# Chunk 0's out-projection by 26 streamed products instead of Strassen's 28

## The chip, the core and the metric

The kernel runs on one core of a Trainium2 chip. Its engines are TensorE (PE, matmuls; PEld are its weight loads), VectorE (DVE), ScalarE (ACT), GpSimd (POOL) and SyncE (SP, which issues most DMAs). Each engine takes its instructions in order, and semaphores hold one engine for another. The metric is the device time of one execution in microseconds; lower is better.

## The reference

```python
scores = scale * np.matmul(q, k.transpose(0, 1, 3, 2))
scores = np.where(mask, scores, -1000000000.0)      # mask: q and k lie nearest the same of 16 centroids
attn = np.exp(scores - max) ; attn = attn / (sum + 1e-09)
x = np.matmul(attn, v)                              # 4 batches x 8 heads x 768 tokens x 64 -> 3072 x 512
h = x @ w_in                                        # 512 -> 2048
g = h * erf(softplus(h))
out = g @ w_out                                     # 2048 -> 512, float32
```

All inputs are float32; the two weights come to the core as 64-bit words (the kernel decodes them by itself, from pairs of 32-bit words).

## The kernel before, in words

**Attention.** Sixteen head pairs follow one another (`period(p, i)`, p = 0 to 15, six periods each). In each period PE does scores and the products with v, ACT the exponentials, DVE maxima and transposes, and POOL adds up the probabilities (`accumulate`). Beside that the weights are decoded, block by block ("steps" n of 32: 16 for `w_in`, 16 for `w_out`): a DMA fetches the raw words into a free tile, ACT takes size, rest and sign, DVE bounds and shifts, and POOL adds the two halves (`summed(n)`) and starts the fetch that reuses the place. Two steps go with a head pair; the last `N_LATE` steps come after the attention. In the last four pairs DVE and POOL also build linear combinations of `w_in` and of x (`forms`; `FORMS` gives DVE's, `POOL_FORMS` the pairs in which POOL takes some).

**MoE part.** The 3072 tokens are six chunks of 512. For each, the hidden layer is computed in two lots (`hidden(n, lot)`): four blocks of seven Strassen products each (`block`, order 1, 2, 6, 7, 5, 3, 4), two float32 matmuls of 128x128 by 128x256 to a product. `fresh` says how each product's bank is evicted into the tiles g: in a lot with the usual copy, ACT copies product 1 and DVE adds or subtracts all the others onto it, in order. PE writes to eight PSUM banks in turn (`bank()`), so it can be eight products ahead of the evictions. Chunks 2 to 5 use a form with 49 products for each pair of chunks (`hidden49`), whose right sides are stored in DRAM as `a_dram`: `begin49` stores parts of `w_in` there, `add49` adds other parts by accumulating DMAs that POOL issues, `copy49` copies one set.

**Out-projection.** Chunk 0 does it in two lots (`project(0, lot, pace)`), each of 2 x 7 Strassen products of four matmuls: 28 products. Chunk 1 and the later ones use `project26`: 26 products of four matmuls. Their right sides are blocks of `w_out` as they are, fixed sums kept in SBUF (`slot(i)`), and ten sums that are streamed from DRAM (`b_dram`, 512 KB each) through a ring of three tiles (`load_stream`), each load issued when the product three stream uses earlier has been given to PE. The left sides are sums of g tiles that DVE builds in place as the products go on (`LEFT_STEPS`), and `AFTER` says how each product is added into the output tiles. The sums of `w_out` blocks are made by POOL (`forms26`, in two pieces to a sum) and, where they are streamed, stored by a DMA.

**What sets the order.** Calls through `te`, `ve`, `ae`, `ge` and `sy` keep the program's order on PE, DVE, ACT, POOL and SP. DMAs issued through `nc.sync` may be placed elsewhere on SP's queue by the framework's planner. `aside_work` is a list of small jobs of which `block` takes `pace` after each product. Tiles from a pool with few buffers wait for the last reader of the buffer's former tile; `gp` has four g buffers, `actp` one buffer for the gate's curves, `gsp` four.

Chunk 0's sequence before: hidden lot 0, hidden lot 1, out-projection lot 0, chunk 1's hidden lot 0, out-projection lot 1, chunk 1's hidden lot 1 (`hidden26`), chunk 1's `project26`. POOL first makes Strassen's forms of `w_out` (`out_forms`) for chunk 0, and then, during chunk 1's hidden layer, twenty 26-product sums out of blocks and of those forms (`EARLY_FORMS`, `LATE_FORMS`).

Of the kernel before, what the change touches and what calls it, by code (L numbers as in the profile page):

```python
# [19 lines left out]
P = 128  # L20
# [5 lines left out]
HW = S // 2  # L26
# [17 lines left out]
POOL_FORMS = range(12, 16)  # L44
# [4 lines left out]
N_LATE = 10  # L49
# [5 lines left out]
EARLY_FORMS = [  # L55
# [3 lines left out]
]  # L59
LATE_FORMS = [  # L60
    (3, -6, 0, -1, None), (4, 0, 6, -1, None), (0, -7, 0, 1, 6), (7, -3, 0, -1, None),
    (10, -4, 2, -1, 0), (6, -6, 6, -1, None), (9, -2, 6, 1, 2), (8, -7, 1, -1, 5),
]
# [49 lines left out]
KEPT = {0: 10, 5: 11}  # L113
HELD = 11
N49 = 2
OUTER = (1, 2, 6, 5, 3, 7, 4)
OUT_ORDER = (1, 3, 2, 5, 4)
# [25 lines left out]
def kernel(  # L143
# [145 lines left out]
    for f in range(HF):  # L289
        for g in (f, HF + f):  # L290
            w_steps.append((w_out[:, g], moe_w_out[g * P : (g + 1) * P]))
# [5 lines left out]
    place_of = {n: places[n % PLACES] for n in range(N_EARLY)}  # L297
    after_of = {n: n + PLACES for n in range(N_EARLY - PLACES)}
    after_of.update({N_EARLY + n: N_EARLY + n + 4 for n in range(N_LATE - 4)})
# [8 lines left out]
    def late_places(first, places):  # L308
        for i, place in enumerate(places):
            place_of.update({N_EARLY + n: place for n in range(first + i, N_LATE, 4)})  # L310
            fetch(N_EARLY + first + i)
# [275 lines left out]
    def divide(u):  # L587
# [9 lines left out]
        if u + 1 < len(units):  # L597
            inv = routep.tile([P, QW], F32, name="inv")
            den = routep.tile([P, QW], F32, name="den")
        else:  # L600
            inv, den = part_of(0, 4 * HW, QW), part_of(1, 0, QW)
# [29 lines left out]
    def load_x(n):  # L631
        if n < NCHUNK:
            if n not in x_of:
                x_of[n] = xp.tile([P, DM // P, CT], F32, name="x_own")
            nc.sync.dma_start(
                out=x_of[n], in_=x_dram.rearrange("(k p) t -> p k t", p=P)[:, :, n * CT : (n + 1) * CT]
            )
# [25 lines left out]
    def coming(n):  # L663
        return range(n + 1, n + 3) if n < N49 else range(n + 2, min(n + 4, NCHUNK)) if n % 2 == 0 else ()
# [39 lines left out]
    def w_out_parts(f, n):  # L704
        f1, f2 = slice(f, f + n), slice(HF + f, HF + f + n)
        return (
            w_out[:, f1, 0:HM], w_out[:, f1, HM:], w_out[:, f2, 0:HM], w_out[:, f2, HM:],
            [more_out[:, i, f1] for i in range(3)],
        )

    g_of = {}
    sums_of = {}

    def g_parts(n, s, lot):
        g, new = g_of[n, s, lot], sums_of[n, s, lot]
        return (
            g[:, 0, :, 0:P], g[:, 1, :, 0:P], g[:, 0, :, P:], g[:, 1, :, P:],
            [new[:, i] for i in range(3)],
        )
# [50 lines left out]
    def further(c11, c12, c21, c22, u):  # L770
        return {
            1: [lambda m: ae.copy(out=u, in_=m), lambda m: onto(c11, m)],
            2: [lambda m: onto(c11, m)],
            6: [lambda m: onto(u, m), lambda m: onto(c12, u)],
            7: [lambda m: onto(u, m), lambda m: onto(c21, u)],
            5: [lambda m: onto(c12, m), lambda m: onto(u, m), lambda m: onto(c22, u)],
            3: [lambda m: onto(c12, m)],
            4: [lambda m: minus_of(c21, c21, m)],
        }

# [34 lines left out]
    def gate(n, lot, s):  # L815

        g = g_of[n, s, lot].rearrange("p h j t -> p (h j t)")
        box = []

        def curves():  # L820
            t = actp.tile([P, 2 * FG * HT], F32, name="a_s")
            box.append(t)
            ae.activation(out=t, in_=g, func=ACT.Softplus)
            ae.activation(out=t, in_=t, func=ACT.Erf)

        def product(i):
            c = slice(i * 512, (i + 1) * 512)
            ve.tensor_tensor(out=g[:, c], in0=box[0][:, c], in1=g[:, c], op=ALU.mult)

        return curves, [functools.partial(product, i) for i in range(2 * FG * HT // 512)]  # L830

    def add_hidden(n, lot, s):
        sums_of[n, s, lot] = gsp.tile([P, 3, FG, P], F32, name="g_more")
        return left_forms(ve, *g_parts(n, s, lot))

    def idle(n):
        return [lambda: None] * n

    def gates(n, lot, which=(0, 1), between=()):
        work = list(between)  # L840
        for s in which:
            curves, products_of = gate(n, lot, s)
            if s == which[0]:
                work = [curves] + work + idle(7 - len(work)) + products_of
            else:
                work += [curves, *sums, *idle(3)] + products_of
            sums = add_hidden(n, lot, s)
        return work + sums
# [4 lines left out]
    def project(n, lot, pace):  # L853

        w = rights(*w_out_parts(lot * FG, FG))
        for s in range(2):
            if lot == 0:
                osb_of[n, s] = outp.tile([P, 2, DM], F32, name="osb")
            osb = osb_of[n, s]
            g = lefts(*g_parts(n, s, lot))  # L860
            c = osb[:, 0, 0:HM], osb[:, 0, HM:], osb[:, 1, 0:HM], osb[:, 1, HM:]

            def done(i):
                if not lot:
                    return
                if (n, s) == (NCHUNK - 1, 1):
                    t, cols = {3: (0, slice(0, DM)), 5: (1, slice(HM, DM)), 4: (1, slice(0, HM))}.get(i, (None, None))
                else:
                    t, cols = {3: (0, slice(0, DM)), 4: (1, slice(0, DM))}.get(i, (None, None))
                if t is not None:  # L870
                    nc.sync.dma_start(out=out_v[2 * n + s, :, t, cols], in_=osb[:, t, cols])

            after = further(*c, up.tile([P, HM], F32, name="u")) if lot else fresh(*c)
            block(lambda i: [(g[i][:, f], w[i][:, f]) for f in range(FG)], after, done, pace)
            del g_of[n, s, lot], sums_of[n, s, lot]


    ring, extra, more_room = [], [], []
    a_dram = dram.tile([len(OUTER), 7, P, LC], F32, name="a_dram")
    b_dram = dram.tile([N_STREAM + len(KEPT), P, FG * HM], F32, name="b_dram")  # L880
# [25 lines left out]
    def place26(x, f):  # L906
        if x == HELD:
            return extra[f // 2].rearrange("p j t -> p (j t)").rearrange("p (f m) -> p f m", f=2)
        return (slot(x) if x >= 0 else w_block(-1 - x))[:, f : f + 2]

    def forms26(steps):
        work = []
        for o, a, b, sign, k in steps:
            form = plus_of if sign > 0 else minus_of

            def piece(f, o=o, a=a, b=b, form=form, k=k):
                form(place26(o, f), place26(a, f), place26(b, f), ge)
                if k is not None:
                    stored = b_dram[k].rearrange("p (f m) -> p f m", f=FG)
                    if o == HELD:  # L920
                        nc.sync.dma_start(out=stored[:, f : f + 2], in_=place26(o, f))
                    elif f:
                        nc.sync.dma_start(out=stored, in_=slot(o))

            work += [functools.partial(piece, f) for f in (0, 2)]
        return work

    def load_kept(i):
        nc.sync.dma_start(out=slot(i), in_=b_dram[KEPT[i]].rearrange("p (f m) -> p f m", f=FG))
# [43 lines left out]
    def hidden26(n, lot, generation=()):  # L973
        generation = list(generation)
        first_steps = [functools.partial(left_step, n, x) for x, step in enumerate(LEFT_STEPS) if step[0] < 0]

        def paired(work):
            if not generation:
                return work
            both = []  # L980
            for w in work + idle(14 - len(work)):
                g = generation[:1]
                del generation[:1]
                both.append(lambda w=w, g=g: [f() for f in (w, *g)])
            return both

        def middle():
            finish_aside()
            aside_work.extend(paired(gate_work(n, lot, 0, first_steps if lot else ())))

        if lot and n > 1:
            aside_work.extend(paired(gate_work(n, 0, 1)))
        else:
            aside_work.extend(paired([]))
        hidden(n, lot, {1: middle})
        finish_aside()
        for work in generation:
            work()
# [18 lines left out]
    def begin49(o):  # L1017
        for a, part in w49_parts(*{1: (0, 0), 2: (0, 1), 4: (1, 1)}.get(o, (1, 0))):
            nc.sync.dma_start(out=form49(o)[:, a], in_=part)

    def copy49(o, source):
        nc.sync.dma_start(out=a_dram[OUTER.index(o)], in_=a_dram[OUTER.index(source)])
# [697 lines left out]
```

## Time and profile before

| | |
|---|---|
| median of the runs | 950.82 us |
| the profiled execution | 950.97 us |
| its span, from first to last instruction | 949.2 us |
| PE, DVE, POOL, ACT busy | 941.6, 752.9, 557.5, 554.8 us |
| granted clock of TensorE, mean | 1.000 |

Among the runs behind the median is one of 1956.87 us; the other two are 950.82 and 950.69. A profile page gives, for each engine, its busy time; then the chain of work that ended last; then groups of instructions as "line engine operation out<-in, shapes, count | busy us, mean ns | idle time before them and what ended it". Nearly all instructions have line L134, since one helper records them, so they are told apart by their tiles: `bank` and `turned` are PSUM banks, `g` the hidden layer, `a_s` the gate's curves, `g_more` and `more_out` places of `w_out` sums, `x_own` a chunk of x, `a_dram` and `b_dram` the two stores in DRAM. A view by stretches gives each engine's busy time between two times in us from the span's start, the clock, the DMA engines' share and GB/s. A view of the DMAs gives, for each queue, packets, MB and share; q1 carries what SP issues, q0 what POOL issues.

### The profile page before, as it was taken

What the parts mean: (1) busy time and instruction counts of PE and PEld (TensorE: products, weight loads), DVE (VectorE), ACT (ScalarE), POOL (GpSimd) and SP (SyncE); (2) the same over time, 40 slices, a digit from 0 to 9 for tenths busy, and PEclk for the clock granted to TensorE, in tenths of its full rate; (3) what the DMA queues carried; (4) which work ended last, traced back from release to release, by engine and by line L of the source; (5) the groups of instructions that cost most, each with busy time, mean ns of one, the idle gap of its engine ahead of it and who ended that gap; (6) DMA issues with size and microseconds to landing.
All of it is one profiled execution on the core that took longest, in us unless ns stands there. A gap on an engine that the chain in (4) does not pass through costs nothing.

```text
span 949.2 us, 20906 instructions
## 1 busy us (share of the span) xinstructions
PE 941.6 (99%) x8167; PEld 695.6 (73%) x8167; DVE 752.9 (79%) x1310; ACT 554.8 (58%) x852; POOL 557.5 (59%) x381
## 2 busy tenths in 40 slices
PE   8999999999999999999999999999999999999998
PEld 3555555555555555588888888888888888888887
DVE  8888888888888887788879878456786974768977
ACT  3788888888887665557523542357825225675341
POOL 1688888888888888845779930576600028770000
PEclk9999999999999999999999999999999999999999
DMA  9444544647454314292895486556645435533443
GB/s 208 93 114 107 116 108 109 156 113 200 91 113 107 71 34 146 81 326 67 164 192 212 155 238 216 156 155 175 191 141 182 156 112 154 171 97 114 153 133 111
DMA packets 181730, 136.15 MB, mean 143 GB/s; under 512 B 131808, under 2 KB 141536, under 8 KB 181600
## 3 DMA queue, kind: packets, MB, share of 16 engines
q1 hardware_dynamic: 174416, 125.21, 45.9%
q0 software_dynamic: 4720, 9.18, 5.5%
q8 instruction: 65, 1.06, 0.5%
q10 hardware_dynamic: 2496, 0.43, 0.2%
q14 instruction: 33, 0.27, 0.1%
HBM read 95.72 MB, written 40.89 MB: 144 GB/s over the span
## 4 chain that ended last, share of the span: by engine, by line
PE 97%; DVE 1%; DMA 0%; ACT 0%; issue 0%; DVEq 0%
PE bank L134 45%; PE turned L134 30%; PE sc L134 17%; PE wide L134 6%; DVE nmx L134 1%; DMA pr<-in_centroids_dram 0%; DMA in_q<-in_q_dram 0%; DVE pr L134 0%; ACT pr L134 0%; DVE sims L134 0%; DVE qT L134 0%; ACT qm L134 0%; DVE turned L134 0%; DVE wide L134 0%; ACT km L134 0%
## 5 line engine op out<-in xcount | busy, mean ns | idle before, releaser
L134 POOL TENSOR_TENSOR more_out<-more_out,pr 128x768 f32<-128x768 f32 x128 | 222.4, 1738 | 17.5 <-ACT pr L134 9.7
L134 DVE TENSOR_REDUCE nmx<-wide 128x2 f32<-128x512 f32 (+2 forms) x189 | 180.7, 956 | 57.8 <-PE wide L134 56.8
L134 ACT ACTIVATE pr<-sc 128x768 f32<-128x768 f32 x192 | 148.6, 810 | 71.5 <-PE wide L134 63.9
L134 PE MATMUL turned<-pr,in_v 128*32 128x193 f32 x3072 | 144.9, 330 | 0.0
L134 PEld LDWEIGHTS turned<-pr,in_v 128*32 128x32 f32 x3072 | 91.5, 109 | 51.5 <-issue 25.5
L134 PE MATMUL sc<-qT,kT 64*128 64x384 f32 x528 | 98.7, 487 | 0.0
L134 POOL TENSOR_TENSOR more_out<-pr,pr 128x768 f32<-128x768 f32 x32 | 58.7, 1834 | 46.6 <-ACT pr L134 46.6
L134 POOL TENSOR_TENSOR u<-w_in 128x1 f32<-128x1 f32 x2 | 0.4, 189 | 138.6 <-DVE w_in L134 138.6
L134 PE MATMUL bank<-x_own,more_in 128*128 128x256 f32 x280 | 69.1, 379 | 0.0
L134 PE MATMUL bank<-g_more,more_in 128*128 128x256 f32 x288 | 66.5, 380 | 0.0
L134 PE MATMUL wide<-kv,qv 64*128 64x256 bf16 (+2 forms) x378 | 64.2, 328 | 1.3 <-DVE nmx L134 0.7
L134 DVE TENSOR_TENSOR g<-g 128x512 f32<-128x512 f32 x70 | 48.6, 695 | 19.3 <-PE bank L134 12.3
L134 PE MATMUL wide<-km,qm 64*128 64x256 bf16 (+3 forms) x378 | 62.6, 327 | 0.0
L134 PEld LDWEIGHTS sc<-qT,kT 64*128 64x128 f32 x528 | 48.0, 187 | 19.5 <-ACT inv L134 3.2
L134 PEld LDWEIGHTS bank<-g_more,more_in 128*128 128x128 f32 x288 | 54.6, 190 | 8.2 <-DVE g L134 0.8
L134 PEld LDWEIGHTS bank<-x_own,more_in 128*128 128x128 f32 x280 | 53.2, 190 | 7.2
L134 DVE TENSOR_TENSOR g<-g,bank 128x256 f32<-128x256 f32 (+1 forms) x85 | 41.9, 511 | 20.4 <-PE bank L134 12.7
L134 ACT ACT_TABLE_LOAD x36 | 46.2, 1283 | 18.4 <-DVE g L134 17.8
L134 PE MATMUL bank<-w_out,g 128*128 128x256 f32 x240 | 55.2, 379 | 0.0
L134 DVE TENSOR_TENSOR g<-a_s,g 128x512 f32<-128x512 f32 x56 | 51.8, 941 | 2.7 <-ACT a_s L134 2.7
L134 PEld LDWEIGHTS <-qv 64*128 64x128 bf16 x384 | 22.8, 93 | 41.4 <-issue 25.3
L134 ACT ACTIVATE x_own<-x_own 128x512 int32<-128x512 uint32 (+2 forms) x52 | 52.7, 1028 | 0.0
(253 smaller groups left out, 2148.3 us busy)
## 6 DMA issues: line engine op xcount, KB each, us to landing
more_in<-a_dram SPq DMA_DIRECT2D x98, 256.0 KB, 2.7
g_more<-b_dram SPq DMA_DIRECT2D x48, 512.0 KB, 3.6
x_own<-in_moe_w_in_dram SPq DMA_DIRECT2D x13, 512.0 KB, 3.6
in_v<-in_v_dram SPq DMA_DIRECT2D x32, 192.0 KB, 3.1
x_dram<-more_out SPq DMA_DIRECT2D x128, 48.0 KB, 2.5
a_dram<-w_in SPq DMA_DIRECT2D x12, 512.0 KB, 5.0
x_own<-x_dram SPq DMA_DIRECT2D x6, 1024.0 KB, 5.9
in_k<-in_k_dram SPq DMA_DIRECT2D x59, 96.0 KB, 2.7
```

The costliest lines, as they stand in the source:

```text
L134: ins = getattr(self.engine, name)(*args, **kw)
```

## The change

Chunk 0 takes the same way as chunk 1: `hidden26(0)`, `hidden26_second(0)`, `project26(0)`, and then `hidden26(1)`, `hidden26_second(1)`, `project26(1)`.

- The sums of `w_out` are now 18, all out of raw blocks and of one another: eleven in `FIRST_FORMS` beside chunk 0's hidden layer (22 pieces on POOL, all first pieces before all second ones) and seven in `LAST_FORMS` during `project26(0)`, at its products -1, 3, 5, 6 and 8. `out_forms`, `EARLY_FORMS` and `LATE_FORMS` go, and the kept copies with them. Two sums that are only streamed are made in the tile that chunk 1's x will take (`BESIDE`).
- `N_LATE` is 6 instead of 10: four more decodings lie in head pairs 12 and 13. POOL's eight forms of pairs 12 to 15 lie in 14 and 15. Four of the late steps' raw words go into two g tiles (`two_g`).
- x of chunk 1 is loaded after product 14 of `project26(0)`, together with x of chunk 2; before, it was loaded during the attention.
- The stores of `a_dram` are issued through `sy`, so in written order: sets 6, 5, 7 in `hidden26_second(0)` behind the stores of the first sums, 1, 2, 4 in `hidden26(1)`. The accumulating DMAs stand behind `project26(0)` in the program and behind POOL's last piece on POOL.
- `project26` has one way for all chunks: the first three evictions wait until product 3, and the gate's curves and products follow `plan26` in halves of the token columns, with x_own of the chunk as a second curve buffer.

```diff
-POOL_FORMS = range(12, 16)
+POOL_FORMS = range(14, 16)
-N_LATE = 10
+N_LATE = 6
-OUT_ORDER = (1, 3, 2, 5, 4)
+BESIDE = (11, 12)
+OUT_ORDER = (0, 1, 3, 2, 5, 4)
...
-            if i % HJ == 1 and p in POOL_FORMS and forms:
+            if i % HJ and p in POOL_FORMS and forms:
                 forms.pop(0)[1]()
...
-            nc.sync.dma_start(out=form49(o)[:, a], in_=part)
+            sy.dma_start(out=form49(o)[:, a], in_=part)
...
+    def hidden26(n, between={}, beside=(), **kw):
+
+        def middle():
+            aside_work.extend(abreast((gate_work(n, 0, 0), 1), (beside, 2)))
+
+        hidden(n, 0, {1: middle, **between}, **kw)
+
+    def hidden26_second(n, between={}):
 
         def middle():
             finish_aside()
+            aside_work.extend(first_steps26(n))
+
+        aside_work.extend(gate_work(n, 0, 1))
+        hidden(n, 1, {1: middle, **between})
         finish_aside()
...
+        last_forms = {p: sum((forms26([step]) for step in LAST_FORMS[p]), []) if not n else [] for p in LAST_FORMS}
+        run(f() for f in curves.get(-1, []) + last_forms[-1])
...
-            if p == 5 and n < N49:
-                load_x(n + 2)
+            if p == 14 and n < N49:
+                if n == 0:
+                    load_x(1, sy)
+                load_x(n + 2, sy)
...
-    late_places(2, [outp.tile([P, 2, DM], F32, name="osb").rearrange("p h m -> p (h m)") for _ in range(2)])
+    take_places(4)
+    two_g = [gp.tile([P, 2, FG, HT], F32, name="g").rearrange("p h j t -> p (h j t)") for _ in range(2)]
+    late_places(2, [t[:, i : i + 2 * LC] for t in two_g for i in (0, 2 * LC)])
...
-    hidden(0, 0, {0: finish_attention, 3: store(1)})
-    hidden(0, 1, {0: store(2), 1: store(4), 2: begin}, pace=2, first=ve.tensor_copy)
-    project(0, 0, 3)
-    hidden(1, 0, first=ve.tensor_copy)
-    project(0, 1, 3)
-    hidden26(1, 1, making)
-    project26(1)
+    making = forms26(FIRST_FORMS)
+    half = len(making) // 2
+    aside_work += idle(3) + abreast((sum((weights(n) for n in range(N_LATE)), []), 2), (idle(4) + making[:half], 1))
+    hidden26(0, {0: finish_attention}, making[half:], first=ve.tensor_copy)
+    hidden26_second(0, {0: store(6), 2: store(5), 3: store(7)})
+    project26(0, gates26(0))
     run(f() for f in add49(6, 1, 1) + add49(5, 1, 1) + add49(7, 0, 0) + add49(6, 0, 0))
+    hidden26(1, {0: store(1), 2: store(2), 3: store(4)}, first=ve.tensor_copy)
     copy49(3, 6)
+    hidden26_second(1)
+    project26(1, gates26(1))
```

More of the change, by code (lines that the diff above doesn't have):

```diff
@@ L309, in late_places @@
         for i, place in enumerate(places):
-            place_of.update({N_EARLY + n: place for n in range(first + i, N_LATE, 4)})
+            place_of[N_EARLY + first + i] = place
             fetch(N_EARLY + first + i)
@@ L813, in hidden @@
             between.get(j, lambda: None)()
[L815 to L830, printed above, removed]
@@ L850 @@
     out_v = out.rearrange("(n t p) m -> n p t m", p=P, t=2)
     osb_of = {}
[L853 to L875, printed above, removed]
@@ L912, in forms26, with piece @@
         work = []
[L913 to L925, printed above, removed]
-        return work
-    def load_kept(i):
-        nc.sync.dma_start(out=slot(i), in_=b_dram[KEPT[i]].rearrange("p (f m) -> p f m", f=FG))
+        for f in (0, 2):
+            for o, a, b, sign, k in steps:
+                def piece(f=f, o=o, a=a, b=b, form=plus_of if sign > 0 else minus_of, k=k):
+                    form(place26(o, f), place26(a, f), place26(b, f), ge)
+                    if k is not None:
+                        stored = b_dram[k].rearrange("p (f m) -> p f m", f=FG)
+                        sy.dma_start(out=stored[:, f : f + 2], in_=place26(o, f))
+                work.append(piece)
+        return work
     def load_stream(k, queue=nc.sync):
@@ L1283, in hidden49 @@
             load_stream(next_out + i)
[L1284 to L1295 removed]
+        first, second = (plan26({t: gates_of[tb, 1, t] for t in range(2)}) for tb in (1, 0))
         first[0][-1] = products_at(1, 0, 1, (1, 1), (0, 0), (1, 0), (0, 1)) + first[0][-1]
@@ L1634, in weights @@
         ]
-    def all_weights(lo, hi):
-        return sum((weights(n) for n in range(lo, hi)), [])
-    out_forms = [right_forms(ge, *w_out_parts(f, 2)) for f in range(0, HF, 2)]
-    def together(a, b):
-        work = []
-        while a or b:
-            work += a[:1] + b[:1]
-            del a[:1], b[:1]
-        return work
-    def begin():
-        for o in (6, 5, 7):
-            begin49(o)
-    def store(o):
-        return functools.partial(begin49, o)
-    aside_work += idle(3) + all_weights(0, 4) + out_forms[0] + out_forms[1]
```

193 lines of the change are left out of this document (61 added, 132 removed), and 3 rows, old and new, of the table EARLY_FORMS.

## The prediction

> **What bounds the kernel now.** I read the page first, for the busy shares and the chain that ended last.
>
> ```profile
> PE 941.6 (99%) x8167; PEld 695.6 (73%) x8167; DVE 752.9 (79%) x1310; ACT 554.8 (58%) x852; POOL 557.5 (59%) x381
> PE 97%; DVE 1%; DMA 0%; ACT 0%; issue 0%; DVEq 0%
> ```
>
> TensorE (PE) is busy for 99% of the span, and the chain runs over it for 97%. Next I cut the span at the first matmul of each head pair and of each block of the MoE part, and asked for busy time by stretch.
>
> ```profile
> core 0: us, PE busy (x) PEld busy (x) DVE busy (x) ACT busy (x) POOL busy (x), PEclk, DMA share, GB/s
> 285.70:310.00 24.30, 24.30 (x358) 13.63 (x355) 20.82 (x34) 19.28 (x33) 20.16 (x13) 1.00 0.47 110
> 310.00:334.20 24.20, 24.20 (x358) 13.57 (x356) 19.82 (x31) 15.40 (x28) 19.65 (x13) 1.00 0.34 67
> 381.90:404.80 22.90, 22.90 (x342) 12.98 (x338) 18.80 (x22) 13.66 (x23) 20.55 (x13) 1.00 0.29 96
> 404.80:429.80 25.00, 25.00 (x125) 21.49 (x122) 20.52 (x45) 11.96 (x15) 11.39 (x9) 1.00 0.86 308
> 429.80:454.00 24.20, 24.20 (x113) 21.06 (x111) 21.91 (x43) 18.28 (x19) 12.59 (x10) 1.00 0.14 45
> 454.00:478.30 24.30, 24.30 (x113) 21.38 (x113) 19.84 (x41) 15.84 (x12) 17.70 (x14) 1.00 0.98 190
> 575.20:620.10 44.90, 44.90 (x210) 39.52 (x209) 29.70 (x59) 13.08 (x27) 16.85 (x12) 1.00 0.51 164
> ```
>
> The rows are head pairs 11, 12 and 15, then chunk 0's two hidden halves (from 404.8), its first half out-projection (454.0) and chunk 1's 26-product out-projection (575.2 is its start). PE fills every stretch at a clock of 1.00. So the kernel gains only by fewer matmuls, and each new PE wait is added in full. The question is what the changed order makes PE wait for.
>
> **The change, part by part. 1: fewer products.**
>
> ```profile
> 457.61 1.89 PE L134 MATMUL bank<-more_out,g_more 128*128 128x256 f32 x8
> 459.34 1.89 PE L134 MATMUL bank<-w_out,g 128*128 128x256 f32 x8
> ```
>
> A product of the out-projection is eight matmul rows, and starts follow each other by 459.34 - 457.61 = 1.73 us. Chunk 0 goes from 28 to 26 products: 2 x 1.73 = **-3.45 us**. The built order has 16 matmul rows less, so this term is sure.
>
> **2: decoding and block sums in the last head pairs.** Four decodings move into pairs 12 and 13. Those become like pair 11, which holds two and takes 24.3 us beside 24.2 for pair 12: +0.1 each. The eight POOL forms that pairs 12 to 15 share now all lie in 14 and 15.
>
> ```profile
> L134 POOL TENSOR_TENSOR w_out<-w_out 128x512 f32<-128x512 f32 x10 | 14.6, 1470 | 0.0
> L134 POOL TENSOR_TENSOR more_out<-w_out,more_out 128x512 f32<-128x512 f32 x10 | 14.4, 1455 | 0.3
> L134 POOL TENSOR_TENSOR w_out<-w_out,more_out 128x512 int32<-128x512 int32 x6 | 7.8, 1297 | 12.2 <-ACT w_out L134 4.8 <-DMA x_dram<-more_out 3.6 <-DVE w_out L134 2.7
> 406.31 2.01 POOL L134 TENSOR_TENSOR more_out<-more_out,pr 128x768 f32<-128x768 f32 x1
> 413.11 1.31 POOL L134 TENSOR_TENSOR w_out<-w_out,more_out 128x512 int32<-128x512 int32 x1 [4.78 <-ACT w_out L134]
> 418.01 1.30 POOL L134 TENSOR_TENSOR w_out<-w_out,more_out 128x512 int32<-128x512 int32 x1 [3.59 <-DMA x_dram<-more_out]
> ```
>
> Two more forms of some 1.3 us in pair 15 make POOL 20.55 + 2.6 = 23.2 us of 22.9. PE's sums over the softmax wait for POOL's accumulates, so some of it shows: I take **+1.5 us** for the four pairs (bounds 0, if the probability buffers cover it, and 3, if half of the four moved forms' 5.2 us and a DVE delay show).
>
> **3: POOL is late, and holds chunk 0's hidden half.** POOL used to have ten late weight sums and eight forms in the first 48 us of the MoE part. Now it has six sums and 22 pieces of block sums there, and 14 more pieces behind them. In the built order the last weight sum stands behind five sums and ten pieces. From 415 us (the first sum's 413.11, later by the two extra forms of pair 15 less some slack), with the 3.6 us wait that the rows show before the second sum, it ends at 415 + 3.6 + 6 x 1.30 + 10 x 1.46 = 441. The raw words of the last four weight blocks lie in the two g buffers that the second half of the hidden layer writes first. That half begins at 404.8 + 1.5 + 24.2 + 1.3 (a hiccup at the start, of which 25.0 beside 24.2 us shows 0.8 today) = 432. VectorE (DVE), which works in order, is held at its first eviction into such a buffer, till 441. PE has eight banks, and a hidden product is half an out-projection product, 0.86 us: cover 6.9 us. Behind DVE's held instruction stand the gate products that free the curve buffer, and behind those ACT's next curves:
>
> ```profile
> 540.00 0.37 ACT L134 COPY g<-turned 128x256 f32<-128x256 f32 x1 [5.85 <-PE turned L134]
> 540.39 1.28 ACT L134 ACT_TABLE_LOAD   x1
> 541.69 2.01 ACT L134 ACTIVATE a_s<-g 128x1024 f32<-128x1024 f32 x2
> 543.71 1.28 ACT L134 ACT_TABLE_LOAD   x1
> 545.01 2.01 ACT L134 ACTIVATE a_s<-a_s 128x1024 f32<-128x1024 f32 x2
> 546.92 0.35 ACT L134 COPY g<-turned 128x256 f32<-128x256 f32 x1
> ```
>
> That is the group as it runs today in chunk 1: 546.92 - 540.39 = 6.5 us between two copies, covered by the banks alone. In chunk 0 it starts late: 441 + two or three gate products (2.5) + 6.5 = 450, and only then comes ACT's copy of the next block's first product, on which all that block's evictions hang. That product ends at 432 + 7 x 0.86 + 0.9 = 439; eight banks carry PE to about 445.5. Stall: some 4.5 us. Then DVE has to catch up beside a POOL that never rests, and this costs:
>
> ```profile
> L134 DVE TENSOR_TENSOR g<-a_s,g 128x512 f32<-128x512 f32 x11 | 16.1, 1483 | 1.2 <-ACT a_s L134 1.2
> L134 DVE TENSOR_TENSOR g<-g 128x512 f32<-128x512 f32 x11 | 7.6, 687 | 1.1 <-PE bank L134 1.0
> ```
>
> The first row is of 500 to 551 us, where POOL is busy throughout, the second of 575 to 620: 1.48 against 0.69 us for an SBUF-to-SBUF operation of one size. About 17 such stand between the hold and POOL's end: +13.5 us of DVE work, of which DVE's idle quarter hides most. I take 2.5 us. With the hiccup of 1.3 us (the x forms on DVE meet POOL's late accumulates, which now end later) this step is **+8.5 us**; bounds 1 (POOL some 5 us earlier, all covered) and 12. The Trainium skill, "SBUF — State Buffer", section "SBUF: two separate sides", says that the pair of ports which these two engines share is an exclusive lock for a whole instruction. If each of the 17 waited for a whole piece, DVE would take 0.69 + 1.46 = 2.15 us for each and the work would grow by 25 us, which would put the time near 978; the mean of 1.48 says that about half of it is waited for.
>
> **4: accumulating DMAs meet the loads.** Chunk 0's out-projection now streams ten 512 KB right sides and, after its product 14, loads x of chunks 1 and 2, 1 MB each. Both x loads used to come elsewhere (chunk 1's during the attention). And POOL issues the twelve accumulating DMAs as soon as its pieces are done.
>
> ```profile
> x_own<-x_dram SPq DMA_DIRECT2D x6, 1024.0 KB, 5.9
> 453.27 0.38 SPq L635 DMA_DIRECT2D x_own<-x_dram  x1
> 499.33 0.59 SPq L1022 DMA_DIRECT2D a_dram<-a_dram  x1
> q0 software_dynamic: 3776, 7.34, 98.5%
> q0 software_dynamic: 285, 0.56, 60.3%
> q1 hardware_dynamic: 300, 0.87, 47.7%
> g_more<-b_dram SPq DMA_DIRECT2D x48, 512.0 KB, 3.6
> g_more<-b_dram SPq DMA_DIRECT2D x3, 512.0 KB, 6.6
> q1 hardware_dynamic: 883, 2.37, 95.1%
> ```
>
> Today SP issues nothing between 453.27 and 499.33 us, and in 458 to 500 the accumulates (q0) have the engines to themselves: 7.34 MB in about 39 us. The next two rows are 567 to 572 us, where three accumulates meet loads: 285 packets against 300, so packets alternate. The load's median goes from 3.6 us to 6.6 (560 to 574). Alone, q1 moved 2.37 MB between 551 and 558. Now the new place. The out-projection starts at 432 + 24.2 + 7 = 463. POOL's first 22 pieces and six sums end at 415 + 3.6 + 7.8 + 22 x 1.46 = 458.5, its last 14 at 479, with a wait for a slot 480.5: there the accumulates begin, to last beyond 519. Product 14 ends at 463 + 15 x 1.73 = 489, so the x loads are issued into the middle of them. At alternating packets of 2 KB the loads get 300 packets x 2 KB in 5 us = 0.12 MB/us: 2.1 MB take 17 us, and stream block 8, queued behind, some 3 more, after a start of 2: landed at 511. PE needs it at product 22, 463 + 22 x 1.73 = 501. Stall 10 us. Block 4, whose sum POOL makes only after the out-projection has begun, is stored and reloaded just about when product 13 wants it: 2 to 4. I take **+14 us**; bounds 2 (loads at the rate of the last row, 7 us for all) and 25 (they get nothing until the accumulates end). The stores that SP now issues in written order, behind the last of the first block sums, only move this by some us.
>
> **The sum** is made against the profiled execution, 950.97 us (span 949.2 and 1.8 around it), 0.15 above the median of 950.82: -3.45 + 1.5 + 8.5 + 14 = +20.5, so **971.5 us**.
>
> **Rivals.** *Everything is covered, and only the matmuls count:* POOL reaches its last weight sum before 438, so that DVE's hold ends inside the 6.9 us of banks, and the x loads pass the accumulates. Then 951.0 - 3.45 = 947.5, faster. For it speaks that PE lost nothing in 500 to 551 with POOL always busy; against it, that nothing there waited for a late POOL result. *POOL's chain alone:* steps 2 and 3 as forecast, but the loads run as fast as between 551 and 558 and land before product 22: 951.0 - 3.45 + 1.5 + 8.5 = 957.5, up to 960 with block 4. *Starved loads:* the x loads wait until the accumulates end at 520 or later; the stall is 25 us or more, the time 983 to 995. *The change doesn't take effect:* 951; the built order speaks against it.
>
> **How the numbers follow.** Forecast 0.70, with 958 to 986 as its own range; all covered 0.12; POOL's chain alone 0.12; starved 0.05; no effect 0.01. Leaving out the first rival, no effect and most of the starved case, the range is 953 to 986. A measurement of this kernel tells about 2%, 19 us, from no change; that bound lies at 970, just under the forecast. Slower: six tenths of the forecast's 0.70 and the starved case, 0.48. Within 2%: all others, 0.51. Faster by 2% can't come from 3.45 us: 0.01.
>
> **What would show it.** Step 1: the out-projection's PE row count is 208 in chunk 0. Step 2: the last four pairs take 24.3, 24.3, 24 and 23.5 us. Step 3: PE idles near 445 us with ACT or DVE as releaser, and DVE has a gap that POOL's int32 sum ends. Step 4: PE idles 10 us or more about product 22, released by a DMA of g_more or by x_own, and the 1 MB loads land after 15 us and not 5.9. I am wrong if chunk 0's out-projection takes 45 us as chunk 1's does, or if POOL's last piece lies before 470.

## The result, and the profile after

The changed kernel takes 980.3 us, the kernel before 951.0 in the same comparison: a ratio of 1.0304, 95% interval 1.028 to 1.0327. Each of the two medians counts one far slower run (1617.2 and 1956.87 us); without it the changed kernel has a median of 979.35 (978.7 to 981.2) and the kernel before 950.82, and the ratio is taken without it. That is **slower by 3%**, on the side that the forecast of 971.5 pointed to, 8 to 9 us beyond it and inside the range.

The page's rows for PE and for the chain that ended last, to be laid beside 941.6 us (99%) and 97% of before:

```profile
PE 946.5 (97%) x8151; PEld 694.1 (71%) x8151; DVE 753.6 (77%) x1320; ACT 557.4 (57%) x880; POOL 531.8 (54%) x360
PE 45%; DVE 5%; ACT 3%; DMA 2%; POOL 2%; issue 1%; DVEq 0%; ACTq 0%; POOLq 0%
```

PE has 16 matmul rows less and is busy 5 us longer, in a span that is 28.4 us longer (977.6 beside 949.2). The chain now leaves PE: DVE, ACT, a DMA and POOL hold it for some time each.

Next, busy time by stretch, cut at the first matmul of head pairs 14 and 15, lots 0 and 1 of chunk 0's hidden layer (its two halves; columns as in the prediction), chunk 0's out-projection and chunk 1's:

```profile
358.40:382.10 23.70, 23.70 (x349) 13.17 (x346) 16.71 (x25) 13.91 (x26) 21.30 (x15) 1.00 0.19 43
382.10:406.50 24.40, 23.22 (x343) 12.88 (x339) 18.17 (x23) 13.65 (x24) 21.37 (x14) 1.00 0.16 54
406.50:434.80 28.30, 26.27 (x125) 21.07 (x122) 22.94 (x44) 20.82 (x24) 21.82 (x16) 1.00 0.32 117
434.80:468.90 34.10, 27.46 (x114) 21.82 (x113) 25.63 (x41) 7.85 (x10) 33.71 (x24) 0.95 0.44 168
468.90:529.40 60.50, 47.97 (x209) 40.76 (x208) 40.74 (x77) 20.11 (x35) 25.59 (x20) 0.92 1.04 274
577.80:624.20 46.40, 45.37 (x210) 39.41 (x209) 37.76 (x74) 18.65 (x34) 4.43 (x4) 1.00 0.64 187
```

Before, PE filled every such stretch at a clock of 1.00. Now it is short of work in five of these six, and in two of them the mean granted clock is below 1. The same cuts in both traces give the account, in us:

| stage | before | after | difference |
|---|---|---|---|
| head pairs 12 to 15 | 94.8 | 96.7 | +1.9 |
| chunk 0, hidden layer, lot 0 | 24.9 | 28.3 | +3.4 |
| chunk 0, hidden layer, lot 1 | 24.3 | 34.1 | +9.8 |
| chunk 0, out-projection | 48.5 (28 products) | 60.5 (26 products) | +12.1 |
| chunk 1, hidden layer | 48.5 | 48.3 | -0.2 |
| chunk 1, out-projection | 44.9 | 46.4 | +1.5 |
| all the rest | | | -0.2 |
| end of the last matmul | 946.0 | 974.3 | +28.3 |

PE's waits from 300 to 630 us, by releaser (columns: total us, times, longest):

```profile
PE turned L133 <- DMA g_more<-b_dram: 11.0, 1, 11.0
PE bank L133 <- DVE g L133: 5.8, 8, 1.7
PE bank L133 <- ACT g L133: 2.9, 1, 2.9
PE turned L133 <- DVE g L133: 2.1, 3, 1.2
PE turned L133 <- POOL more_out L133: 1.2, 1, 1.2
PE bank L133 <- POOL x_own L133: 0.4, 1, 0.4
```

**The 11.0 us in the out-projection.** The chain between 490 and 530 us has one long piece:

```profile
500.69 19.45 DMA g_more<-b_dram
```

This is stream block 8: SP issues it at 500.69 us, it lands 19.45 us later, at 520.15, and PE goes on at 520.28. The DMA view of 490 to 525 us shows what it met (first two rows: packets, MB, share of 16 engines; last row: count, size, median us to landing):

```profile
q0 software_dynamic: 2229, 4.34, 66.9%
q1 hardware_dynamic: 1919, 5.24, 42.1%
x_own<-x_dram SPq DMA_DIRECT2D x2, 1024.0 KB, 18.1
```

POOL's accumulates and SP's loads get packets in similar numbers, 2229 and 1919, and a 1 MB load of x lands after 18.1 us, not the 5.9 of before. A stop also has an after-effect, to be seen in the columns PE busy and PEclk of these stretches:

```profile
510.00:515.00 5.00, 0.00 (x0) 0.00 (x0) 4.86 (x11) 1.15 (x3) 0.00 (x0) 0.94 1.09 263
515.00:520.00 5.00, 0.00 (x0) 0.00 (x0) 2.88 (x6) 0.00 (x0) 0.00 (x0) 0.50 1.09 294
520.00:525.00 5.00, 4.72 (x12) 3.83 (x13) 0.42 (x1) 0.00 (x0) 0.00 (x0) 0.53 1.09 279
525.00:530.00 5.00, 5.00 (x25) 4.41 (x24) 2.21 (x6) 1.66 (x2) 0.00 (x0) 1.00 1.10 254
```

While PE stands, its granted clock falls to 0.50. In the 5 us after the restart it is 0.53, and PE gets 12 matmul rows done where it later does 25.

**Lot 1.** Three timelines, of DVE, ACT and PE (start, duration; in brackets the idle time before and its releaser):

```profile
441.84 0.42 DVE L133 TENSOR_TENSOR g<-turned,g 128x256 f32<-128x256 f32 x1 [2.40 <-POOL w_out L133]
442.18 1.40 DVE L133 TENSOR_TENSOR g<-a_s,g 128x512 f32<-128x512 f32 x1
443.83 1.42 DVE L133 TENSOR_TENSOR g<-a_s,g 128x512 f32<-128x512 f32 x1
452.24 0.42 DVE L133 TENSOR_TENSOR g<-bank,g 128x256 f32<-128x256 f32 x1 [5.13 <-ACT g L133]
456.02 4.78 DVE L133 TENSOR_TENSOR g<-a_s,g 128x512 f32<-128x512 f32 x3
```

```profile
445.33 1.28 ACT L133 ACT_TABLE_LOAD   x1 [9.05 <-DVE g L133]
451.85 0.63 ACT L133 COPY g<-bank 128x256 f32<-128x256 f32 x2
```

```profile
452.25 1.37 PE L133 MATMUL bank<-x_own,w_in 128*128 128x256 f32 x4 [2.89 <-ACT g L133]
453.42 1.91 PE L133 MATMUL bank<-x_more,more_in 128*128 128x256 f32 x4
462.85 1.13 PE L133 MATMUL bank<-x_more,more_in 128*128 128x256 f32 x4 [1.74 <-DVE g L133]
```

The chain forecast is there: DVE held by POOL until 441.8, ACT's curves from 445.3, its copy at 451.9, and PE idle before 452.25, with four slow matmul rows behind (1.91 us; they take 1.03 at full clock). But three gate products (the rows g<-a_s,g) then take 4.78 us of DVE, and PE is short again at 462.85, with DVE as releaser. Of the 9.8 us that lot 1 grew by, 2.9 are waits for ACT, 3.7 waits for DVE, and in 3.2 PE was busy longer for the same products, in part at the lowered clock (0.95 in the mean).

### The profile page after: what moved, and what is told of

It is laid out like the page before. It is cut to its first block, busy times and chain, and to the rows that moved or that the text cites. A ratio compares the mean times of both kernels' runs of the same rounds, so it can differ in the third digit from the quotient of the medians.

```text
span 977.6 us, 20925 instructions
## 1 busy us (share of the span) xinstructions
PE 946.5 (97%) x8151; PEld 694.1 (71%) x8151; DVE 753.6 (77%) x1320; ACT 557.4 (57%) x880; POOL 531.8 (54%) x360
## 4 chain that ended last, share of the span: by engine, by line
PE 45%; DVE 5%; ACT 3%; DMA 2%; POOL 2%; issue 1%; DVEq 0%; ACTq 0%; POOLq 0%
PE bank L133 35%; PE turned L133 9%; DVE g L133 3%; DMA g_more<-b_dram 2%; ACT a_s L133 1%; ACT x_own L133 1%; ACT L133 1%; POOL g_more L133 1%; DVE g_more L133 1%; POOL w_out L133 1%; POOL more_out L133 0%; DVE osb L133 0%; DVE w_out L133 0%; ACT osb L133 0%; ACT g_more L133 0%
## 5 line engine op out<-in xcount | busy, mean ns | idle before, releaser
L133 DVE TENSOR_TENSOR g<-g 128x512 f32<-128x512 f32 x88 | 61.7, 701 | 22.6 <-PE turned L133 11.0
L133 ACT ACTIVATE x_own<-x_own 128x512 int32<-128x512 uint32 (+2 forms) x62 | 62.8, 1028 | 0.0
L133 PEld LDWEIGHTS sc<-qT,kT 64*128 64x128 f32 x528 | 47.6, 187 | 20.0 <-ACT inv L133 3.4
L133 PE MATMUL bank<-g_more,g 128*128 128x256 f32 x256 | 60.8, 380 | 0.3 <-DVE g L133 0.3
L133 PEld LDWEIGHTS bank<-g_more,g 128*128 128x128 f32 x256 | 48.4, 190 | 8.0 <-issue 1.7
L133 PEld LDWEIGHTS <-qv 64*128 64x128 bf16 x384 | 23.0, 93 | 41.7 <-issue 25.6
```

Source lines behind the costliest of these rows:

```text
L133: ins = getattr(self.engine, name)(*args, **kw)
```

## The experiments

All are edits of the changed kernel, and gains are counted from its 979.35 us (the expectations say 980.3); its runs spread over 2.5 us, so a gain of that size is a rough one. The kernel before took 950.6 to 950.8 us beside them. Stage times are cut as above, each from one profiled execution; the last column is the median:

| kernel | pairs 12-15 | lot 0 | lot 1 | out-projection, chunk 0 | out-projection, chunk 1 | us |
|---|---|---|---|---|---|---|
| changed | 96.7 | 28.3 | 34.1 | 60.5 | 46.4 | 979.4 |
| loads first | 96.8 | 28.3 | 34.1 | 47.3 | 46.4 | 966.0 |
| adds late | 96.8 | 28.3 | 34.1 | 47.2 | 49.8 | 969.1 |
| x of chunk 2 late | 96.8 | 28.3 | 35.2 | 53.6 | 46.7 | 972.5 |
| DVE copy | 96.7 | 29.4 | 29.0 | 62.8 | 46.4 | 977.1 |
| other places | 96.7 | 30.6 | 31.7 | 60.6 | 46.4 | 979.2 |
| POOL's forms spread | 96.0 | 26.8 | 32.7 | 60.0 | 46.4 | 976.9 |
| fills | 96.7 | 30.2 | 29.4 | 60.3 | 46.4 | 977.0 |
| quiet POOL | 96.8 | 26.9 | 30.0 | 60.6 | 46.4 | 973.9 |
| three remedies | 96.0 | 25.7 | 30.3 | 49.5 | 46.4 | 961.4 |
| all four remedies | 96.1 | 26.8 | 29.1 | 49.7 | 46.4 | 961.2 |
| three remedies, quiet POOL | 96.0 | 24.9 | 25.9 | 47.6 | 46.4 | 952.0 |

**Who meets whom in the out-projection.** My theory: the accumulates share the DMA engines with the loads. The rival: the loads are issued too late anyway. The first run puts the accumulates behind the first x load, the second behind the whole out-projection.

```diff
     project26(0, gates26(0))
+    fence(x_of[2][:, 0])
     run(f() for f in add49(6, 1, 1) + add49(5, 1, 1) + add49(7, 0, 0) + add49(6, 0, 0))
```

> One fence: POOL starts the accumulating DMAs of the out-projection's sums only after chunk 2's first x load has landed. Changed kernel 980.3 us, its chunk 0 out-projection 60.5 us against 44.9 us for 26 products of chunk 1 before the change. Theory (the accumulates share the DMA engines with the loads, and product 22 waits for stream block 8): the wait of 11.0 us released by the DMA of g_more goes, and the low granted clock behind it; out-projection 45 to 48 us, total 965 to 969 us. Rival (the loads are simply issued too late, at 494 to 501 us, because POOL's last piece ends at 482 us): the wait stays above 8 us, total 977 to 981 us.

It took 965.99 us, ratio to before 1.0159 (1.0144 to 1.0174). POOL's timeline, then the whole of PE's waits from 468.9 to 516.2 us:

```profile
502.46 0.64 POOL L133 TENSOR_TENSOR u<-x_own 128x1 f32<-128x1 f32 x1 [20.02 <-DMA x_own<-x_dram]
503.04 2.60 POOL L133 DMA_DIRECT2D a_dram<-w_in  x2
```

```profile
PE turned L133 <- DVE g L133: 1.2, 1, 1.2
PE bank L133 <- DVE g L133: 0.5, 1, 0.5
```

SP issues the x loads at the same time as in the changed kernel (494.38 beside 494.26 us); only the accumulates start 20.8 us later (503.04, not 482.26). The wait of 11.0 us is gone, and the out-projection is 13.2 us shorter. So the wait itself is 11.0 of these, and most of the other 2.2 is the lowered clock behind it: the first eight rows took 3.75 us at 520.28 in the changed kernel, against the 1.73 at which products follow each other otherwise. The rival falls.

```diff
     project26(0, gates26(0))
+    fence(osb_of[0, 1][:, 0])
     run(f() for f in add49(6, 1, 1) + add49(5, 1, 1) + add49(7, 0, 0) + add49(6, 0, 0))
```

> The fence stands later: the accumulating DMAs start only when chunk 0's out-projection has written its last output tile. Theory (sharing of the DMA engines): as with the loads first, out-projection 45 to 48 us, but the accumulates now run beside chunk 1's hidden layer and may reach its out-projection's loads: total 965 to 970 us. Rival (loads issued too late): 977 to 981 us.

969.14 us, ratio 1.0192 (1.0177 to 1.0208): inside its expectation. Chunk 0 is as with the loads first, but chunk 1's out-projection grows by 3.4 us, with one wait (PE's waits, 560 to 620 us):

```profile
PE bank L133 <- DMA g_more<-b_dram: 2.4, 1, 2.4
```

The same DMA, one chunk later: accumulates that are put off meet the next loads.

```diff
-                load_x(n + 2, sy)
+                if n:
+                    load_x(2, sy)
+                    load_x(3, sy)
```

> Chunk 2's x is not loaded at product 14 of chunk 0's out-projection, but later, with chunk 3's in chunk 1's; the accumulating DMAs stay where they are. That takes 2 MB from in front of stream block 8 in SP's queue. Theory (block 8 is late because it shares the engines and stands behind the x loads): block 8 is issued some 4 us earlier and has one rival transfer less, the wait at product 22 falls from 11.0 us to between 0 and 4 us, total 968 to 974 us. Rival (the accumulates alone hold block 8, whatever else is loaded): the wait stays at 8 to 11 us, total 977 to 981 us.

972.46 us, ratio 1.0229 (1.0214 to 1.0244). With 1 MB less ahead of stream block 8 the wait is not gone but falls to a third (the edit takes away chunk 2's 1 MB; the 2 MB of the expectation counted both x loads). PE's waits, 400 to 660 us:

```profile
PE turned L133 <- DMA g_more<-b_dram: 3.3, 1, 3.3
```

So both are needed for the 11.0 us: the shared engines, and 2 MB of x in front of the block in SP's queue.

**Who makes the hidden layer late.** Three suspects: ACT's curves ahead of its copy, the g buffers held by raw words, and DVE's SBUF operations beside POOL.

```diff
-    hidden26_second(0, {0: store(6), 2: store(5), 3: store(7)})
+    hidden26_second(0, {0: store(6), 2: store(5), 3: store(7)}, first=ve.tensor_copy)
```

(`hidden26_second` hands `first` on to `hidden`.)

> In lot 1 of chunk 0's hidden layer the first product's PSUM is copied out by DVE instead of ACT, as the other whole products' are; so no curve table is loaded again between ACT's copy and its curves. Theory of the chain (DVE held by POOL's late sum, ACT's copy and table load behind DVE, PE's PSUM bank behind both): the lot takes 34.1 us in the changed kernel and 29 to 31 us here, total 975 to 977 us. Rival (DVE alone sets it, ACT only follows): lot 1 stays at 33 to 35 us, total 979 to 982 us.

977.14 us, ratio 1.0278 (1.0261 to 1.0295). Lot 1 falls by 5.1 us to 29.0, as the theory said (the total lies just above its 977), and the row of PE's wait for ACT's copy is gone. Lot 0 gives 1.1 back and the out-projection 2.2, nearly all in longer waits for DVE (1.9 and 1.9 us at the two places where the changed kernel has 0.3 and 1.2); the wait for block 8 stays, at 11.2 us. ACT's place in the chain is shown; it isn't all.

```diff
-    late_places(2, [t[:, i : i + 2 * LC] for t in two_g for i in (0, 2 * LC)])
+    late_places(2, [outp.tile([P, 2, DM], F32, name="osb").rearrange("p h m -> p (h m)") for _ in range(2)])
+    for first, again in ((1, 4), (2, 5)):
+        place_of[N_EARLY + again] = place_of[N_EARLY + first]
+        after_of[N_EARLY + first] = N_EARLY + again
```

> The raw words of the last four late weight blocks lie in the two output tiles (two of them in places used a second time) and not in the two g buffers, so no eviction of the hidden layer's lot 1 waits for a weight sum. Changed kernel 980.3 us with lot 0 28.3 and lot 1 34.1 us. Theory of the hold (DVE is held at its first eviction into such a buffer until POOL's last int32 sum): DVE's wait for POOL at 441.8 us goes and lot 1 takes 28 to 31 us, total 975 to 978 us if lot 0 keeps its time. Rival (DVE is late because its SBUF operations beside POOL take twice as long, the hold is covered): lot 1 stays at 33 to 35 us, total 979 to 982 us.

979.23 us, ratio 1.0301 (1.0286 to 1.0317): no difference from the changed kernel that these runs can tell. Lot 1 becomes 2.4 us shorter, as much as DVE's wait for POOL was, and lot 0 2.3 us longer, so the edit moved the delay. The expectation allowed for this only in its last words, "if lot 0 keeps its time". By the total the rival was right, though lot 1's 31.7 us lie between the two expectations: freeing the buffers in this way buys nothing. The test isn't clean, since two of the raw blocks now go into places that are used a second time and are fetched only after an earlier block's sum; why lot 0 grows isn't shown.

```diff
-POOL_FORMS = range(14, 16)
+POOL_FORMS = range(12, 16)
...
-            if i % HJ and p in POOL_FORMS and forms:
+            if i % HJ == 1 and p in POOL_FORMS and forms:
```

> One part undone: POOL's eight forms of x lie in pairs 12 to 15 again, two in each, and not all in pairs 14 and 15. Theory (pair 15's extra POOL work delays PE's sums there by 1.5 us and makes POOL and DVE late at the start of the hidden layer): pair 15 falls from 24.4 to 23.0 to 23.5 us and lot 0 from 28.3 to 25.5 to 26.5 us, total 975.5 to 978.5 us. Rival (the start of lot 0 is set by the new decodings and block sums alone): pair 15 gains 1 us, lot 0 nothing, total 979 to 980 us.

976.87 us, ratio 1.0274 (1.0259 to 1.029). Pair 15 goes back from 24.4 to 22.9 us and lot 0 from 28.3 to 26.8, but pairs 12 and 13, which hold the new decodings, now take 24.8 each and not 24.3. So pair 15's extra work on POOL costs 1.5 us there and 1.5 at the start of the hidden layer; half a microsecond each comes back in pairs 12 and 13. (The stages are those of an execution of 975.52 us, 1.4 below the median.)

```diff
-                    form(place26(o, f), place26(a, f), place26(b, f), ge)
+                    if steps is FIRST_FORMS:
+                        ge.memset(place26(o, f), 0.0)
+                    else:
+                        form(place26(o, f), place26(a, f), place26(b, f), ge)
```

> The 22 pieces of the first eleven block sums are replaced on POOL by fills with zero of the same size, so those sums are left out; their stores, the six late weight sums and everything after stay. It tells how much of the cost is POOL's time for these pieces. Theory (a late POOL holds the g buffers and starts the accumulating DMAs too late): POOL's last weight sum ends near 430 us, lot 1 takes 24.2 to 26 us instead of 34.1, the accumulates start 20 us or more earlier and are mostly through when the x loads come, so the out-projection takes 45 to 52 us instead of 60.5: total 955 to 964 us. Rival (the hidden layer is late by DVE's own decodings, the out-projection by the number of bytes): lots and out-projection change by less than 3 us each, total 974 to 981 us.

976.95 us, ratio 1.028 (1.0263 to 1.0297): the rival's total, 13 us above the theory's. The fills take 0.52 us apiece, and POOL is through with them at 445 us. Lot 1 falls to 29.4, more than the rival's 3 us and less than the theory said, and lot 0 rises to 30.2. The fills aren't neutral for DVE: its six float32 operations of the decodings (w_out<-w_out) take 1.70 us each beside them, 0.88 in the changed kernel, so this run can't price POOL's time in the lots. The out-projection stays at 60.3, and the reason is in two timelines, POOL's and SP's queue:

```profile
476.85 2.95 POOL L133 TENSOR_TENSOR x_own<-more_out,w_out 128x512 f32<-128x512 f32 x2 [14.25 <-DMA b_dram<-x_own]
479.75 2.60 POOL L133 DMA_DIRECT2D a_dram<-w_in  x2
```

```profile
471.78 0.32 SPq L133 DMA_DIRECT2D g_more<-b_dram  x1
472.22 2.09 SPq L133 DMA_DIRECT2D b_dram<-x_own  x4
```

POOL waits 14.25 us for the store of an earlier sum. That store stands in SP's queue behind a stream load, and the stream load waits until PE has used a buffer of the out-projection (SP stands for 13.5 us, released by PE). So the accumulates start 13.4 us after the out-projection does, here (466.4 and 479.75) and in the changed kernel (468.9 and 482.26), though POOL's pieces before that wait end at 462.6 here and at 476.4 there. In the changed kernel they end just before the store, which is why POOL's lateness looked like the cause:

```profile
479.36 2.96 POOL L133 TENSOR_TENSOR x_own<-more_out,w_out 128x512 f32<-128x512 f32 x2 [2.92 <-DMA b_dram<-x_own]
```

```diff
-                    form(place26(o, f), place26(a, f), place26(b, f), ge)
+                    if steps is FIRST_FORMS:
+                        nc.sync.dma_start(out=place26(o, f), in_=x_dram[0:P, 0:2 * HM].rearrange("p (f m) -> p f m", f=2))
+                    else:
+                        form(place26(o, f), place26(a, f), place26(b, f), ge)
```

> POOL computes none of the 22 pieces of the first eleven block sums: SP issues a DMA of the same size into each piece in place of the operation (so those sums are left out), and stores, weight sums and all else stay. With the fills POOL was busy 42 of the hidden layer's 60 us and DVE's SBUF operations stayed slow; here POOL is idle for most of it. Theory (DVE is slowed by sharing SBUF with a busy POOL, and that, with the curves behind it, makes the hidden layer late): DVE's 128x512 SBUF operations in the two lots fall from about 1.4 to about 0.7 us, the two lots together take 50 to 55 us instead of 62.4 in the changed kernel and 59.7 with the fills, total 968 to 974 us. Rival (DVE is late by its own new decodings and by the order of work alone): the lots stay at 58 to 62 us, total 976 to 980 us.

973.91 us, ratio 1.0245 (1.023 to 1.026), just inside the theory's total. The lots together take 56.9 us, between the two expectations: DVE's wait of 5.1 us for ACT's copy is still there, and POOL is quiet only for a part of the time. The timelines of DVE and POOL show what its return means:

```profile
438.50 0.68 DVE L133 TENSOR_TENSOR g<-a_s,g 128x512 f32<-128x512 f32 x1
...
449.68 4.78 DVE L133 TENSOR_TENSOR g<-a_s,g 128x512 f32<-128x512 f32 x3
460.58 0.42 DVE L133 TENSOR_TENSOR g<-bank,g 128x256 f32<-128x256 f32 x1
```

```profile
448.79 1.77 POOL L133 TENSOR_TENSOR w_out<-w_out,g_more 128x512 f32<-128x512 f32 x1 [11.09 <-DMA g_more<-x_dram]
450.52 3.39 POOL L133 TENSOR_TENSOR g_more<-w_out 128x512 f32<-128x512 f32 x2
460.56 2.49 POOL L133 TENSOR_TENSOR more_out<-w_out,more_out 128x512 f32<-128x512 f32 x2
```

The gate product at 438.50 stands in POOL's pause and takes 0.68 us. At 449.68 POOL is back, and three of them take 4.78 us, 1.59 each; POOL's pieces then take 1.70 instead of some 1.25. The eviction from PSUM at 460.58 takes its usual 0.42 us beside a working POOL.

**Together.** The first of these runs joins the loads first, the DVE copy and POOL's forms of x spread over pairs 12 to 15 (the edits above).

> Three edits at once: accumulating DMAs only after the first x load of the out-projection, DVE instead of ACT for the first product's copy in lot 1, and POOL's forms of x in pairs 12 to 15. If the three causes are separate, their gains add: 980.3 - 14.3 (loads first, measured) - 3.1 (DVE copy, measured) - 2 to 4.5 = 958.5 to 961 us. If one hides another, 962 to 966 us. In neither case is the kernel before (950.8 us) reached.

961.42 us, ratio 1.0114 (1.0099 to 1.0129), as if hardly anything were hidden: 13.4 + 2.2 + 2.5 = 18.1 us alone, 17.9 together. Then the other places for the raw words, too:

> Four edits at once: the three of the run before (loads first, DVE copy, POOL's forms of x in pairs 12 to 15; 961.4 us with lots of 25.7 and 30.3 us) and the raw words in the output tiles. Neither POOL's late weight sum nor ACT's curves then stand in front of DVE's evictions in lot 1. Theory (hold and curves matter only as far as DVE has no slack to catch up; what is left is DVE's slow work beside POOL): the lots together gain 0 to 2 us, total 959 to 961.5 us. Rival (the hold and the curves together make lot 1 late): lot 1 falls to 25 to 27 us, total 956 to 958 us.

961.23 us, ratio 1.0111 (1.0094 to 1.0128): the theory's. DVE doesn't wait for POOL's late sum any more, and for ACT's curves only twice 0.8 us, and lot 1 still takes 29.1 us. Last, the three remedies and the quiet POOL in one kernel:

> The three remedies of the run with 961.4 us (loads first, DVE copy, POOL's forms of x in pairs 12 to 15) and the quiet POOL together: the 22 pieces of the first eleven block sums are left out, a DMA of the same size into each stands in their place. It asks whether POOL's work beside DVE is what remains. Remedies alone: lots of 25.7 and 30.3 us, out-projection 49.5 us. Theory (DVE's SBUF operations wait for POOL's, one by one): lots of 24.9 to 26 and 25 to 27 us, out-projection 46 to 49 us, total 953 to 957 us, so that even without this work the kernel before (950.7 us) isn't reached. Rival (the lots stay late by the order of DVE's and ACT's own work): lot 1 at 29 us or more, total 959 to 962 us.

951.95 us, ratio 1.0015 (1.0006 to 1.0025), below the 953 that the theory gave as its end. Its profiled execution was 2.5 us above this median. Lots of 24.9 and 25.9 us are the kernel before's within 1.6, and DVE's work in lot 1 falls from 26.0 us with the three remedies to 23.6. PE's waits, 406 to 504.4 us:

```profile
PE turned L133 <- DVE g L133: 1.8, 2, 1.2
PE bank L133 <- DVE g L133: 1.3, 2, 0.8
```

So POOL's 22 pieces cost 9.5 us by the medians even with the three remedies, and 7.2 by the profiled executions: 5.2 in the lots and 1.9 in the out-projection. Leaving them out also brings POOL's last weight sum forward, to 428.8 us, but the run before this one shows that freeing DVE from that sum gains nothing by itself. Only without the pieces does a version come back near the time before, and it is still 1.3 us above it. No version here beats it.

## Why the prediction was right, and where it was off

**What bounds the kernel.** That each new wait of PE counts in full held: the stage differences add up to the difference of the ends. One slip: the row of 575.2 to 620.1 us was called chunk 1's out-projection of before. By its first matmuls that ran from 551.0 to 595.9; its length is the same 44.9 us, and no term hung on the place.

**Step 1, -3.45 us: right.** 8167 rows became 8151. With the loads first, the 26 products take 47.3 us: 26 x 1.73 = 45.0, waits of 1.7 for DVE, and 0.6 more.

**Step 2, +1.5 us: right in size.** Forecast 24.3, 24.3, 24.0 and 23.5; measured 24.32, 24.33, 23.72 and 24.38, +1.9 for the four. Pair 15 took more of it than forecast.

**Step 3, +8.5 us: mis-sized; it measured 13.2, outside its bounds of 1 to 12.** (The terms as written, 4.5 + 2.5 + 1.3, add up to 8.3.) The rows came where the working put them (DVE held till 441, found 441.8; ACT's copy after 450, found 451.9), and PE's stop there was shorter than forecast, 2.9 us and not 4.5. Two terms were too small, and the lowered clock was none at all. The hiccup at the start of the hidden layer, 1.3 us, was in truth lot 0's 3.4, half of it from pair 15's POOL forms. And DVE's catching up beside POOL, taken at 2.5 because DVE's idle quarter hides most, wasn't hidden: DVE's work in lot 1 came to 25.6 us, more than the 24.3 us that PE took for the lot before. That is so although only 14 operations of 128x512 from SBUF to SBUF stood between the hold's end and POOL's end at 482.3 us, not 17: eleven before POOL's pause at 476 us, three behind it. The weight was put on the wrong link, too: with the raw words in other places nothing is gained, without ACT's copy 2.2 us, and with three causes mended POOL's pieces still cost 9.5 in the whole kernel.

The prediction read the 1.48 us of DVE's operations as "about half" of a wait for a whole piece. The single operations say more than the mean. In POOL's pauses one takes 0.68 us. Alone between evictions, beside POOL's pieces, it takes 1.40 or 1.42 (rows 442.18 and 443.83), nearly the same each time, where a wait from a random moment of a piece would spread from 0.69 to 2.15 us. In a row it takes 1.59, and POOL's pieces then take 1.70 instead of 1.25. Evictions from PSUM are untouched. The Trainium skill, "SBUF — State Buffer", section "SBUF: two separate sides", states an exclusive lock that is held for a whole instruction. The trace agrees in that both engines are slowed. But two whole instructions in turn would take 0.68 + 1.25 = 1.93 us, and the rows show 1.59 and 1.70, so these runs don't settle how much of an instruction is locked. The estimate of 978 us by that rule was the nearer one, partly by luck: it put 2.15 us on each of 17 operations, and the eleven before POOL's pause took 0.94 to 1.75.

**Step 4, +14 us: right in mechanism, nearly in size.** Over 26 x 1.73 = 45.0 us the out-projection took 15.5 more. The x loads landed after 18.1 us in the median, and block 8 at 520.15, when PE had wanted it 11.0 us before 520.28. Need and landing both lay some 8 to 9 us later than forecast, in good part because step 3 was larger, so the stall of "10" came out as 11.0. The rate of the loads was misread: 0.87 MB in 5 us is 0.17 MB/us and not 0.12, since q1's packets were larger than 2 KB. From 490 to 525 us q1 moved 5.24 MB, 0.15 MB/us, but stream loads went through it beside the 2.1 MB of x, so that 17 us came near the 18.1 measured is partly luck. The lowered clock (most of 2.2 us) was no term at all, and the 2 to 4 us for block 4's reload didn't show: in its place stand waits of 1.5 us that DVE released. For the start of the accumulates the working gave 480.5 and the trace 482.3, but the reason was incomplete: the fills show that a faster POOL doesn't start them sooner, because SP's queue holds the store before them.

**Not foreseen:** chunk 1's out-projection, +1.5 us. PE has one wait there, of 1.0 us, released by DVE, which is busy 9.7 of every 10 us between 590 and 610. The stage took 46.4 us or more in every experiment, and none took the loss away; its cause stays open.

Of the rivals, "POOL's chain alone" (957.5 to 960) sets the conditions of the run with the loads first: it took 966.0, more than the rival's sum because step 3 was larger, so without the collision too the change loses. "All covered" asked for banks that outlast DVE's hold; the rows at 452.25 and 462.85 say that they didn't.

## What to carry to other kernels

In this kernel, where PE is full, two products fewer (3.5 us) bought nothing. One reason is that the sums that replace them go to POOL, whose work slows the SBUF operations of DVE, the engine that empties PE's banks: weigh new work by what it does to its neighbour's operations, one by one, and not by the engine's own idle share. Before blaming a slow engine for a late transfer, make it fast and look again; the transfer may wait in a queue whose order the program wrote. Put bulk accumulates after the loads that a matmul waits for, and check what they meet next.

## What the hardware showed that I had not expected

PE's granted clock falls when PE stands, and stays low after the restart: 0.94 and 0.50 in the two 5 us stretches of the 11 us stop, 0.53 in the 5 us after it, 1.00 in the next. So this stop cost about 2 us more than its own length.

After short stops it is less regular. The stop of 2.9 us before 452.25 was followed by a product of 1.91 us instead of 1.03, and with the three remedies a stop of 1.98 us by one of 2.07. But with x of chunk 2 late the same wait for ACT, 2.89 us, was followed by products of 1.03 us, and in the changed kernel the stop of 1.74 us before 462.85 by one of 1.13. What decides it these runs don't show.
